# Casting V in the DMA, regrouping q and k as 64 rows of nine tokens, and a new order of loads in an attention and SwiGLU kernel

## Chip, cores and metric

One NeuronCore of one Trainium2 chip. The metric is device time in microseconds (us) of the whole launch, lower is better.

## What is computed

Causal attention with a selective bias, for 8 batches of 8 heads, 576 tokens and head size 64, and then a SwiGLU feed-forward block (FFN) on the 4608 rows that come out:

```python
cum  = np.cumsum(np.maximum(s, 0.0), axis=-1)
bias = -(cum[:, :, :, None] - cum[:, :, None, :])
scores = q @ k.T / sqrt(64) + minimum(bias, 0)     # causal
attn = softmax(scores) @ v                         # (8, 8, 576, 64)
x = attn.transpose(0, 2, 1, 3).reshape(4608, 512)
g = x @ w_gate                                     # 512 x 1536
out = (g * sigmoid(g) * (x @ w_val)) @ w_out       # 1536 x 512
```

Inputs and output are float32; the kernel multiplies in bfloat16.

## The kernel before

Heads are worked in 16 half-batches of four. For each, k and q are loaded, cast to bfloat16, and turned so that the head dimension lies on partitions. Half-batches 0 to 4 are turned by TensorE. From half-batch 5 on they go through scratch buffers in memory and a transposing DMA. Four small bias copies per half-batch (from the tile HL into the tiles KQ) add the rows that carry the cumulative sum. Scores of a head cannot start before its q, its k and its bias copy are all in KQ.

```python
J = 6                      # tokens per row: 576 = 96 rows of 6
NP = S // J                # partitions used by a q or k tile
def load_one(hb, name):    # hb: half-batch
    t = raw.tile([NP, HB, J, D], FP32, tag="raw" + name)          # two buffers
    nc.sync.dma_start(t, SRC[name][0][b, g*HB:(g+1)*HB].rearrange("h (p j) d -> p h (j d)", j=J))
def cast_one(hb, name, r, eng): ...        # NP x (2 heads * J * 64), float32 to bfloat16
def pe_transpose(hb, name, r, engs):
    for j in range(J):
        nc.tensor.transpose(ps[:, j, :], ct[:, r, j]..., ident[0:NP, 0:NP])
    # two copies from PSUM into KQ
...
nc.sync.dma_start(s_sb, ...); load_qk(0); load_qk(1); load_v(0, range(5))     # SyncE's queue
for r in range(NR): cast_one(0, "k", r, nc.gpsimd)                             # first casts on Pool
for r in range(NR): cast_one(0, "q", r, nc.gpsimd)
aug(0, [nc.scalar, nc.gpsimd, nc.scalar, nc.gpsimd])                           # bias copies
...
def side(h, step):         # called in the middle of each head; h is the half-batch
    ...                    # h == 0, step 3: load_qk(2)
    if h >= 2 and h + 3 < NHB and step == 0: load_qk(h + 3)
    ...                    # V: load on SyncE, cast on Pool, one batch ahead
# in attn_items, for half-batches 2, 3 and 4:
    if h > 3: aug(h, SP4)                      # bias copies of half-batch 4 are queued here
    for nm in ("k", "q"): cast_one(h, nm, 0, nc.gpsimd)
    ...                                        # then the transposes, then the heads
hook = {21: [lambda: load_qk(4)]}              # half-batch 4 is loaded late, by the first FFN tile
```

Batch 0 runs alone up to the "FFN start". After that the FFN of each batch's rows is woven between the heads of later ones; its first tile takes heads 8 to about 17. In the profile PE is TensorE, DVE VectorE, ACT ScalarE, POOL GpSimd (called Pool here) and SP SyncE; tps are TensorE's transposes, sc the scores, av the PV products, and pg, pv and py the FFN's gate, value and output products; ck and cq are the cast tiles, ks and qs the scratch buffers.

The softmax here doesn't subtract the row's maximum and nothing guards it: scores larger than these inputs give would overflow.

Of the kernel before, what the change touches and what calls it, by code (L numbers as in the profile page):

```python
# [12 lines left out]
FP32 = mybir.dt.float32  # L13
# [6 lines left out]
def kernel(  # L20
# [23 lines left out]
    J = 6  # L44
# [4 lines left out]
    WCH = 384  # L49
# [40 lines left out]
    WO = [const.tile([128, 3, DM], BF16, name=f"wo{j}") for j in range(4)]  # L90
# [12 lines left out]
    with tc.manual_schedule():  # L103
# [17 lines left out]

        def load_v(b, cs):
            if 0 in cs:
                loaded["v", b] = raw.tile([128, NCH, H, D], FP32, tag="rawv", bufs=1, name="rawv")
            t = loaded["v", b]
            for c in cs:
                n = 128 if c < 4 else TAIL
                nc.sync.dma_start(
                    t[0:n, c, :, :],
                    v[b, :, c * 128 : c * 128 + n, :].rearrange("h p d -> p h d"),  # L130
                )

        nc.sync.dma_start(s_sb, s.rearrange("b h n -> (b h) n"))
        load_qk(0)
        load_qk(1)
        load_v(0, range(5))

        PAIR_ONE = 1.0019378662109375
# [6 lines left out]
        nc.scalar.activation(warm, warm, AF.Exp)  # L145
        make_identity(nc, ident)
        nc.vector.memset(one_s, 1.0)
        nc.vector.memset(HL[:, 2:4, 0, :].bitcast(FP32), -1.005844116210937500)
        nc.vector.memset(HL[:, 0:2, 1, :].bitcast(FP32), PAIR_ONE)
        for e in range(2):  # L150
            nc.gpsimd.memset(aug_rows(0, e)[:, 1, :], PAIR_ONE)
            nc.vector.memset(aug_rows(0, e)[:, 0, :], 0.0)
        nc.gpsimd.memset(aug_rows(1, 0)[:, 1, :], PAIR_ONE)

# [4 lines left out]
        nc.vector.tensor_copy(HL[:, 2:4, 1, :], HL[:, 0:2, 0, :])  # L159

# [61 lines left out]
        def cast_v(b, c, eng):  # L222
            n = 128 if c < 4 else TAIL
            eng.tensor_copy(VT[b % 2][0:n, c, :, 0:D], loaded["v", b][0:n, c, :, :])  # L224

        def w_load(kind, j):
            dst = {"g": WG, "v": WV, "o": WO}[kind][j]
            if kind == "o":
                src_ap = moe_w_out[j * 384 : (j + 1) * 384, :].rearrange(
# [79 lines left out]
        def x_pe(pr):  # L309
# [16 lines left out]
            1: ("g", 2), 2: ("v", 2), 3: ("g", 3), 4: ("v", 3),  # L326
            5: ("o", 0), 6: ("o", 1), 7: ("o", 2), 8: ("o", 3),
        }

        def side(h, step):  # L330
# [3 lines left out]
            if h == 0:  # L334
                if step == 0:
                    for r in range(NR):
                        cast_one(1, "k", r, nc.gpsimd)
                        cast_one(1, "q", r, nc.gpsimd)
                if step == 1:
                    for nm in ("k", "q"):  # L340
                        pe_transpose(1, nm, 0, (nc.vector, nc.vector))
                if step == 2:
                    for nm in ("k", "q"):
                        pe_transpose(1, nm, 1, (nc.vector, nc.vector))
                if step == 3:
                    for c in range(5):
                        cast_v(0, c, nc.vector)
                    load_qk(2)
                return
            if h == 1:  # L350
                if step == 0:
                    aug(2, SP4)
                    load_v(1, range(5))
# [20 lines left out]
            if bn < B:  # L374
                if h % 2 == 0:
                    if step == 2:
                        load_v(bn, (0, 1))
                    if step == 3:
                        load_v(bn, (2, 3, 4))
                else:  # L380
                    if step == 1:
                        cast_v(bn, 0, nc.gpsimd)
                        cast_v(bn, 1, nc.gpsimd)
                    if step == 2:
                        cast_v(bn, 2, nc.gpsimd)
                        cast_v(bn, 3, nc.gpsimd)
                    if step == 3:
                        cast_v(bn, 4, nc.gpsimd)
# [174 lines left out]
```

## Time and profile before

| | before |
|---|---|
| time, median (range) of 3 runs | 427.5 us (427.38 to 428.12) |
| span of the profiled execution, granted clock | 425.2 us, 0.984 |
| first scores / first PV product / FFN start | 16.3 / 27.7 / 45.5 us |
| first gate product of the second FFN tile | 106.4 us |
| from there to the end | 318.8 us |

The prediction below shows how the page, the windows and the chain lead to these anchors. The last two rows cut the rest: "middle" is FFN start to the second FFN tile's first gate product (pg), "tail" is what follows.

### The profile page before, as it was taken

The page shows a single profiled execution, that of the slowest core. Times are in us where ns is not written, and L with a number is a line of the kernel's source. Part 1 is how long each engine was busy: PE and PEld are TensorE (multiplying, and loading weights), DVE is VectorE, ACT ScalarE, POOL GpSimd, SP SyncE. Part 2 cuts the span into 40 slices and gives each one's busy share as a digit, 9 for nine tenths or more (in the row PEclk, how much of TensorE's full clock was granted, in tenths as well). Part 3 has the DMA queues.
Part 4 walks back from the last instruction along what each step waited for, and adds up shares of the span by engine and source line. Part 5 has one row for each costly group of instructions (what it writes and reads, how often), then busy time and mean ns, then how long its engine had stood idle before and what let it go on. Part 6 is the DMA issues. An engine that isn't in the chain of part 4 may idle for free.

```text
span 425.2 us, 8041 instructions
## 1 busy us (share of the span) xinstructions
PE 387.1 (91%) x3058; PEld 215.3 (51%) x3112; DVE 255.1 (60%) x502; ACT 208.3 (49%) x418; POOL 142.1 (33%) x255
## 2 busy tenths in 40 slices
PE   1487788978999999999999999999999999999996
PEld 1265445545555555555555555555555554444442
DVE  7485558551697369636963796378637651861760
ACT  1454375654555455545554555555555642333321
POOL 5978133552335333533443344334411110000000
PEclk9999799997999999999999999999999999999999
DMA  8999998475796678467956994784720002002002
GB/s 191 205 244 195 199 227 179 94 209 151 165 198 114 175 194 192 105 188 172 207 101 190 185 199 102 186 183 90 105 83 2 2 25 76 0 2 100 2 1 99
DMA packets 92943, 56.71 MB, mean 133 GB/s; under 512 B 65600, under 2 KB 88208, under 8 KB 92904
## 3 DMA queue, kind: packets, MB, share of 16 engines
q1 hardware_dynamic: 86864, 51.40, 53.5%
q0 software_dynamic: 6016, 4.78, 7.0%
q8 instruction: 24, 0.39, 0.4%
q14 instruction: 15, 0.12, 0.1%
q10 hardware_dynamic: 24, 0.02, 0.0%
HBM read 37.90 MB, written 15.93 MB: 127 GB/s over the span
## 4 chain that ended last, share of the span: by engine, by line
PE 87%; DVE 4%; DMA 4%; issue 2%; ACT 1%; POOL 1%; SPq 0%; ACTq 0%
PE py L467 22%; PE pg L443 22%; PE pv L456 21%; PE sc L253 10%; PE av L286 8%; DVE kq L220 3%; PE xps L318 3%; DMA kq<-HL 2%; DMA rawq<-in_q_dram 2%; ACT pt L261 1%; DVE ot L302 1%; POOL cq L177 0%; DVE pp L450 0%; ACT th L448 0%; DVE rc L301 0%
## 5 line engine op out<-in xcount | busy, mean ns | idle before, releaser
L261 ACT ACTIVATE pt<-sc 128x512 bf16<-128x512 f32 (+1 forms) x256 | 117.5, 505 | 60.6 <-PE sc L253 60.3
L450 DVE SCALAR_TENSOR_TENSOR pp<-th,pg 128x512 bf16<-128x512 bf16 x108 | 74.1, 686 | 61.9 <-ACT th L448 61.5
L443 PE MATMUL pg<-xt,wg 128*128 128x512 bf16 x414 | 109.8, 381 | 1.3 <-issue 0.3
L456 PE MATMUL pv<-xt,wv 128*128 128x512 bf16 x412 | 109.6, 380 | 1.0
L448 ACT ACTIVATE th<-pg 128x512 bf16<-128x512 f32 x108 | 64.5, 597 | 92.5 <-PE pg L443 91.8
L467 PE MATMUL py<-wo,ht 128*128 128x512 bf16 x416 | 104.9, 383 | 1.0 <-issue 0.2
L253 PE MATMUL sc<-kq 128*128 128x128 bf16 (+4 forms) x576 | 77.7, 251 | 12.6 <-DVE kq L503 4.7
L265 POOL TENSOR_SCALAR_AFFINE_SELECT pt<-pt 128x512 bf16<-128x512 bf16 x64 | 40.6, 635 | 130.1 <-ACT pt L261 129.8
L461 DVE TENSOR_TENSOR ht<-pp,pv 128x512 bf16<-128x512 bf16 x108 | 73.9, 684 | 8.5 <-PE pv L456 0.9
L253 PEld LDWEIGHTS <-kq 128*128 128x128 bf16 x576 | 47.6, 102 | 46.8 <-issue 8.5
L467 PEld LDWEIGHTS <-ht 128*128 128x128 bf16 x432 | 38.5, 99 | 35.8 <-issue 1.1
L456 PEld LDWEIGHTS <-wv 128*128 128x128 bf16 x432 | 38.7, 98 | 35.2 <-issue 0.8
L443 PEld LDWEIGHTS <-wg 128*128 128x128 bf16 x432 | 38.3, 98 | 35.6 <-issue 0.5
L286 PE MATMUL av<-vt,pt 128*128 128x65 bf16 x960 | 51.4, 198 | 4.0 <-DVE ot L302 2.7
L286 PEld LDWEIGHTS <-pt 128*128 128x128 bf16 x960 | 42.6, 100 | 24.5 <-issue 5.0
L475 ACT ACTIVATE ysb<-py 128x512 f32<-128x512 f32 x36 | 21.5, 597 | 47.1 <-PE py L467 46.0
L270 POOL TENSOR_SCALAR_AFFINE_SELECT pt<-pt 128x64 bf16<-128x64 bf16 x64 | 15.3, 240 | 60.9 <-ACT pt L261 60.8
L301 DVE RECIPROCAL rc<-av 128x5 f32<-128x5 f32 x64 | 12.1, 189 | 37.5 <-PE av L286 37.5
L302 DVE TENSOR_TENSOR ot<-av,rc 128x320 bf16<-128x320 f32 x64 | 31.4, 491 | 2.2
L322 DVE COPY xt<-xps 128x64 bf16<-128x64 bf16 (+7 forms) x32 | 9.7, 304 | 37.3 <-PE xps L318 37.3
L177 POOL CAST ck<-rawk 96x768 bf16<-96x768 f32 x32 | 26.1, 835 | 3.6 <-DMA rawk<-in_k_dram 3.6
L224 POOL CAST vt<-rawv 128x512 bf16<-128x512 f32 (+1 forms) x35 | 23.0, 675 | 9.8 <-DMA rawv<-in_v_dram 9.8
(42 smaller groups left out, 168.6 us busy)
## 6 DMA issues: line engine op xcount, KB each, us to landing
rawk<-in_k_dram SPq DMA_DIRECT2D x16, 576.0 KB
rawq<-in_q_dram SPq DMA_DIRECT2D x16, 576.0 KB
out_dram<-ysb SPq DMA_DIRECT2D x36, 256.0 KB
rawv<-in_v_dram SPq DMA_DIRECT2D x32, 256.0 KB
ks<-ck SPq DMA_DIRECT2D x11, 288.0 KB
qs<-cq SPq DMA_DIRECT2D x11, 288.0 KB
wg<-in_moe_w_gate_dram POOLq DMA_DIRECT2D x4, 384.0 KB, 9.9
wv<-in_moe_w_val_dram POOLq DMA_DIRECT2D x4, 384.0 KB, 11.4
```

What stands on the lines that cost most here:

```text
L177: eng.tensor_copy(cts[name, hb][:, r].rearrange("p j e d -> p e j d"), loaded[name, hb][:, 2 * r : 2 * r + 2, :, :],)
L253: nc.tensor.matmul(sc[:, o : o + w], T[:, 0, r * S + 128 * tj : r * S + 128 * (tj + 1)], T[:, 1, r * S + lo : r * S + hi], start=True, sto ...
L261: nc.scalar.activation(pt[:, CHUNK_PT[ci] : CHUNK_PT[ci] + o], sc[:, 0:o], AF.Exp, scale=0.125)
L265: nc.gpsimd.affine_select(pt[:, 1088:1600], pt[:, 1088:1600], pattern=[[0, 4], [1, 128]], compare_op=ALU.is_ge, fill=zreg, base=0, channel ...
L286: nc.tensor.matmul(av[:, bi * (D + 1) : (bi + 1) * (D + 1)], pt[:, c0 : c0 + 128], VT[b % 2][:, tj, h, :], start=(tj == 0), stop=(tj == bi),)
L302: nc.vector.tensor_mul(ot[:, :, e * D : (e + 1) * D], av3[:, :, 0:D], rc[:, :, None].to_broadcast([128, NCH, D]),)
L443: nc.tensor.matmul(pg, WG[j][:, c, f0 : f0 + 128], xt[:, c, :], start=(c == 0), stop=(c == 3),)
L448: nc.scalar.activation(th, pg, AF.Tanh, scale=0.5)
L450: nc.vector.scalar_tensor_tensor(pp, in0=th, scalar=1.0, in1=pg, op0=ALU.add, op1=ALU.mult)
L456: nc.tensor.matmul(pv, WV[j][:, c, f0 : f0 + 128], xt[:, c, :], start=(c == 0), stop=(c == 3),)
L461: nc.vector.tensor_mul(ht, pp, pv)
L467: nc.tensor.matmul(py, hts[ft][:, ts_ * 128 : (ts_ + 1) * 128], WO[ft // 3][:, ft % 3, :], start=(ft == 0), stop=(ft == NFT - 1),)
```

## The change

The intent: take V's casts from the engines and V's loads from SyncE's queue, move fewer and longer descriptors for q and k, free the bias copies from waiting behind Pool's casts, and have the first casts done by an engine that is idle at that moment.

```diff
-    J = 6
+    J = 9
-    WCH = 384
+    WCH = 768
         def load_v(b, cs):
-                nc.sync.dma_start(
-                    t[0:n, c, :, :],
+                nc.gpsimd.dma_start(
+                    VT[b % 2][0:n, c, :, 0:D],          # casts on the way
@@ start @@
-        load_qk(0)
+        load_first()                                    # k and q by pairs of heads
         load_qk(1)
-        load_v(0, range(5))
@@ side(), half-batch 0 @@
-                if step == 0: (casts of half-batch 1 on gpsimd)
+                if step < 2:  (casts of half-batch 1 on vector)
-                    load_qk(2)
@@ attn_items @@
                 if first and bh == H:
+                    aug(3, SP4)
+                    load_qk(2)
                     load_qk(3)
-                    aug(3, SP4)
@@ prologue @@
-            cast_one(0, "k", r, nc.gpsimd)
+            cast_act("k", r)                            # ScalarE
+            cast_act("q", r)
-        aug(0, [nc.scalar, nc.gpsimd, nc.scalar, nc.gpsimd])
+        aug(0, [nc.gpsimd] * 4)
-        aug(1, [nc.gpsimd] * 4)
+        aug(1, SP4)
+        load_v(0, range(5))
@@ weaving @@
-            n0 = 0
+            n0 = 6 if tt == 0 else 0                    # six FFN units before head 8
```

(Cut to its core; parenthesised lines sum up several. WCH is the number of columns in one piece of the FFN's weights, SP4 is SyncE's queue for all four bias copies that `aug` issues, and a step is a quarter of a half-batch, one head. The cut leaves out that the weights' pieces are also issued at other heads.)

More of the change, by code (lines that the diff above doesn't have):

```diff
@@ L48 @@
     NFT = DF // 128
-    WCH = 384
+    WCH = 768
+    WKO = 6
     NWCH = DF // WCH
@@ L89 @@
     WV = [const.tile([128, 4, WCH], BF16, name=f"wv{j}") for j in range(NWCH)]
-    WO = [const.tile([128, 3, DM], BF16, name=f"wo{j}") for j in range(4)]
+    WO = [const.tile([128, WKO, DM], BF16, name=f"wo{j}") for j in range(NFT // WKO)]
     KQ = [
@@ L120, in load_qk, with load_first @@
             load_one(hb, "q")
+        def load_first():
+            for name in ("k", "q"):
+                loaded[name, 0] = raw.tile([NP, HB, J, D], FP32, tag="raw" + name, name="raw" + name)
+            for r in range(NR):
+                for name in ("k", "q"):
+                    nc.sync.dma_start(
+                        loaded[name, 0][:, 2 * r : 2 * r + 2, :, :],
+                        SRC[name][0][0, 2 * r : 2 * r + 2, :, :].rearrange(
+                            "h (p j) d -> p h (j d)", j=J
+                        ),
+                    )
         def load_v(b, cs):
-            if 0 in cs:
-                loaded["v", b] = raw.tile([128, NCH, H, D], FP32, tag="rawv", bufs=1, name="rawv")
-            t = loaded["v", b]
             for c in cs:
                 n = 128 if c < 4 else TAIL
-                nc.sync.dma_start(
-                    t[0:n, c, :, :],
+                nc.gpsimd.dma_start(
+                    VT[b % 2][0:n, c, :, 0:D],
                     v[b, :, c * 128 : c * 128 + n, :].rearrange("h p d -> p h d"),
@@ L133 @@
         nc.sync.dma_start(s_sb, s.rearrange("b h n -> (b h) n"))
-        load_qk(0)
+        load_first()
         load_qk(1)
-        load_v(0, range(5))
-        PAIR_ONE = 1.0019378662109375
+        ONES2 = 1.0019378662109375
+        NEGS2 = -1.0058441162109375
         def aug_rows(i, e):
@@ L145 @@
         nc.scalar.activation(warm, warm, AF.Exp)
+        nc.vector.memset(one_s, 1.0)
+        nc.vector.memset(HL[:, 2:4, 0, :].bitcast(FP32), NEGS2)
+        nc.vector.memset(HL[:, 0:2, 1, :].bitcast(FP32), ONES2)
         make_identity(nc, ident)
-        nc.vector.memset(one_s, 1.0)
-        nc.vector.memset(HL[:, 2:4, 0, :].bitcast(FP32), -1.005844116210937500)
-        nc.vector.memset(HL[:, 0:2, 1, :].bitcast(FP32), PAIR_ONE)
         for e in range(2):
-            nc.gpsimd.memset(aug_rows(0, e)[:, 1, :], PAIR_ONE)
-            nc.vector.memset(aug_rows(0, e)[:, 0, :], 0.0)
-        nc.gpsimd.memset(aug_rows(1, 0)[:, 1, :], PAIR_ONE)
+            nc.gpsimd.memset(aug_rows(0, e)[:, 1, :], ONES2)
+            nc.gpsimd.memset(aug_rows(0, e)[:, 0, :], 0.0)
+            nc.scalar.copy(
+                KQ[1][e][64 * (1 - e) : 64 * (1 - e) + 64, 1, :],
+                one_s[:, 0:1].to_broadcast([64, NR * S + 64]),
+            )
+        nc.vector.memset(aug_rows(1, 0)[:, 0, :], 0.0)
         nc.vector.tensor_scalar(s_sb, s_sb, 0.0, 8.0, ALU.max, ALU.mult)
@@ L159 @@
         nc.vector.tensor_copy(HL[:, 2:4, 1, :], HL[:, 0:2, 0, :])
+        for e in range(2):
+            for i in range(2):
+                nc.vector.memset(KQ[i][e][64 * e : 64 * e + 64, :, NR * S :], 0.0)
         def aug(hb, engs):
@@ L220, in pe_transpose @@
                     engs[e].tensor_copy(dst, srcp)
-        def cast_v(b, c, eng):
-            n = 128 if c < 4 else TAIL
-            eng.tensor_copy(VT[b % 2][0:n, c, :, 0:D], loaded["v", b][0:n, c, :, :])
         def w_load(kind, j):
@@ L228, in w_load @@
             if kind == "o":
-                src_ap = moe_w_out[j * 384 : (j + 1) * 384, :].rearrange(
+                src_ap = moe_w_out[j * WKO * 128 : (j + 1) * WKO * 128, :].rearrange(
                     "(c p) n -> p c n", p=128
@@ L325 @@
         wlate = {
-            1: ("g", 2), 2: ("v", 2), 3: ("g", 3), 4: ("v", 3),
-            5: ("o", 0), 6: ("o", 1), 7: ("o", 2), 8: ("o", 3),
+            0: ("g", 0), 1: ("v", 0), 2: ("g", 1), 3: ("v", 1), 6: ("o", 0), 7: ("o", 1),
         }
@@ L334, in side @@
             if h == 0:
-                if step == 0:
-                    for r in range(NR):
-                        cast_one(1, "k", r, nc.gpsimd)
-                        cast_one(1, "q", r, nc.gpsimd)
-                if step == 1:
+                if step < 2:
                     for nm in ("k", "q"):
-                        pe_transpose(1, nm, 0, (nc.vector, nc.vector))
-                if step == 2:
+                        cast_one(1, nm, step, nc.vector)
                     for nm in ("k", "q"):
-                        pe_transpose(1, nm, 1, (nc.vector, nc.vector))
-                if step == 3:
-                    for c in range(5):
-                        cast_v(0, c, nc.vector)
-                    load_qk(2)
+                        pe_transpose(1, nm, step, (nc.vector, nc.vector))
                 return
@@ L352, in side @@
                     aug(2, SP4)
+                    init_vt(1)
+                if step == 1:
                     load_v(1, range(5))
@@ L373, in side @@
             bn = h // 2 + 1
-            if bn < B:
-                if h % 2 == 0:
-                    if step == 2:
-                        load_v(bn, (0, 1))
-                    if step == 3:
-                        load_v(bn, (2, 3, 4))
-                else:
-                    if step == 1:
-                        cast_v(bn, 0, nc.gpsimd)
-                        cast_v(bn, 1, nc.gpsimd)
-                    if step == 2:
-                        cast_v(bn, 2, nc.gpsimd)
-                        cast_v(bn, 3, nc.gpsimd)
-                    if step == 3:
-                        cast_v(bn, 4, nc.gpsimd)
+            if bn < B and h % 2 == 1:
+                if step == 0:
+                    load_v(bn, (0, 1))
+                if step == 1:
+                    load_v(bn, (2, 3, 4))
         def attn_items():
@@ L403, in attn_items @@
                         cast_one(h, nm, 1, nc.gpsimd)
-                    if h == 2:
-                        for c in range(5):
-                            cast_v(1, c, nc.gpsimd)
                     yield kk + 0.01
@@ L468, in ffn_items @@
                         py, hts[ft][:, ts_ * 128 : (ts_ + 1) * 128],
-                        WO[ft // 3][:, ft % 3, :],
+                        WO[ft // WKO][:, ft % WKO, :],
                         start=(ft == 0), stop=(ft == NFT - 1),
@@ L479, in ffn_items, with cast_act, init_vt @@
                 yield 1
-        for r in range(NR):
-            cast_one(0, "k", r, nc.gpsimd)
-        for r in range(NR):
-            cast_one(0, "q", r, nc.gpsimd)
-        aug(0, [nc.scalar, nc.gpsimd, nc.scalar, nc.gpsimd])
-        nc.gpsimd.memset(aug_rows(1, 1)[:, 1, :], PAIR_ONE)
-        for e in range(2):
-            nc.vector.memset(aug_rows(1, e)[:, 0, :], 0.0)
-        pe_transpose(0, "k", 0, (nc.scalar, nc.scalar))
-        pe_transpose(0, "k", 1, (nc.scalar, nc.scalar))
-        pe_transpose(0, "q", 0, (nc.vector, nc.vector))
-        pe_transpose(0, "q", 1, (nc.vector, nc.vector))
-        w_load("g", 0)
-        w_load("v", 0)
-        aug(1, [nc.gpsimd] * 4)
-        w_load("g", 1)
-        w_load("v", 1)
-        for i in range(2):
-            nc.vector.memset(VT[i][:, :, :, D : D + 1], 1.0)
-            nc.vector.memset(VT[i][64:128, 4, :, 0:D], 0.0)
-        for e in range(2):
-            for i in range(2):
-                nc.vector.memset(KQ[i][e][64 * e : 64 * e + 64, :, NR * S :], 0.0)
+        def cast_act(name, r):
+            if r == 0:
+                cts[name, 0] = cp.tile([NP, NR, J, 2, D], BF16, tag="c" + name, bufs=2, name="c" + name)
+            nc.scalar.copy(
+                cts[name, 0][:, r].rearrange("p j e d -> p e j d"),
+                loaded[name, 0][:, 2 * r : 2 * r + 2, :, :],
+            )
+        def init_vt(i):
+            nc.gpsimd.memset(VT[i][:, :, :, D : D + 1], 1.0)
+            nc.gpsimd.memset(VT[i][64:128, 4, :, 0:D], 0.0)
+        for r in range(NR):
+            cast_act("k", r)
+            cast_act("q", r)
+        aug(0, [nc.gpsimd] * 4)
+        for nm in ("k", "q"):
+            pe_transpose(0, nm, 0, (nc.vector, nc.vector))
+        for nm in ("k", "q"):
+            pe_transpose(0, nm, 1, (nc.vector, nc.vector))
+        nc.vector.memset(aug_rows(1, 1)[:, 0, :], 0.0)
+        aug(1, SP4)
+        init_vt(0)
+        load_v(0, range(5))
         at = attn_items()
```

## The prediction

> **What bounds the kernel now.** I read the page's forty slices first, then ten-microsecond windows, then the chain of waits and the timeline of the first 100 us, and last the waits by line. From the page of the kernel before:
>
> ```profile
> PE   1487788978999999999999999999999999999996
> DVE  7485558551697369636963796378637651861760
> POOL 5978133552335333533443344334411110000000
> PEclk9999799997999999999999999999999999999999
> DMA  8999998475796678467956994784720002002002
> ```
>
> From slice 11 on (about 106 us) TensorE is full; Pool and VectorE never are. What can be won lies in the first ten slices. The windows say how much:
>
> ```profile
> 0.00:10.00 10.00, 1.32 (x12) 0.90 (x12) 7.76 (x13) 1.49 (x2) 5.18 (x12) 1.00 0.79 187
> 10.00:20.00 10.00, 3.89 (x27) 2.45 (x27) 4.55 (x12) 5.31 (x10) 9.33 (x15) 1.00 1.26 210
> 40.00:50.00 10.00, 7.49 (x69) 4.77 (x71) 4.29 (x12) 1.19 (x2) 2.65 (x4) 0.66 1.20 204
> 50.00:60.00 10.00, 7.42 (x61) 4.25 (x62) 5.88 (x10) 7.14 (x14) 4.32 (x8) 1.00 1.07 215
> 70.00:80.00 10.00, 7.48 (x77) 4.62 (x77) 6.52 (x12) 7.29 (x14) 3.63 (x6) 1.00 0.51 120
> 90.00:100.00 10.00, 5.93 (x54) 3.73 (x53) 4.25 (x8) 4.74 (x9) 3.19 (x5) 0.76 0.65 171
> 200.00:300.00 100.00, 99.16 (x830) 55.75 (x845) 69.16 (x139) 55.38 (x115) 39.19 (x70) 1.00 0.71 157
> ```
>
> The first two numbers are the stretch and TensorE's busy time in it. In the first 50 us TensorE idles 21.4 us (50 less 1.32, 3.89, 7.89, 8.03 and 7.49); three later windows lose 2.6, 2.5 and 4.1; the hundred from 200 lose 0.8. The last three columns (granted clock, DMA share, GB/s) show the DMA engines saturated at the start. The chain of waits through the start, cut:
>
> ```profile
> 2.09 7.16 DMA rawq<-in_q_dram
> 10.84 6.13 DMA kq<-HL
> 19.47 0.78 POOL ck L177
> 20.97 0.02 issue
> 21.00 0.75 DVE kq L220
> 27.17 0.90 DVE vt L224 x2
> 28.11 0.33 PE av L286 x3
> 45.18 0.33 issue
> 45.52 1.49 PE pg L443 x3
> ```
>
> Three anchors follow: the bias copy (kq<-HL) lands at 16.97 and holds the Pool queue and the first heads; the second half-batch (heads 4 to 7) runs through Pool casts, transposes and VectorE copies from 19.5 to 27; the first PV product starts at 27.7, the FFN at 45.5. From there to 425.2 is 379.7 us, nearly all TensorE.
>
> **What the Trainium skill says.** "DMA: Bandwidth & Descriptors", section "SWDGE vs HWDGE vs iDMA": only GpSimd's queue casts during a DMA. The weights already do this here. "Perfetto Trace Analysis", section "DMA Instruction — SWDGE (GPSIMD)": the recorded length of a Pool DMA is descriptor generation, not the movement. The trace agrees: wg issues take a median of 0.77 us and land after 9.9. "SBUF — State Buffer", section "Door 1: The DMA port swizzle": partitions 0 to 63 reach only 8 of 16 ports, measured there at 196 GB/s for 1 MiB. The 96-row loads here run at 245 to 257 GB/s (windows from 4 to 12 us); a 64-row load has no run yet. "TensorE: Matmul & The Clock Gate", Part 1: an idle array drops to half clock and needs about 3.4 us of work to recover. The trace agrees: the granted clock is 0.50 from 42 to 46 us, where TensorE waits for VectorE between PV products.
>
> **The change part by part.**
>
> 1. V by a casting Pool DMA. It removes 35 Pool casts (23.0 us) and 5 VectorE casts (1.9 us) and takes 40 DMAs off SP. Only two of these are near the path: the VectorE casts at 27.17 and the second batch's Pool casts, which waited 9.8 us for their data and put the ninth head's mask behind them (54.35 us). It adds 40 issues to Pool. A 64-descriptor bias issue takes 0.60, a 384- or 512-descriptor weight issue 0.75 to 0.82; the slope is about 0.4 ns a descriptor, so 1024 descriptors cost about 1.0 us (estimate). Five in a row are 5 us, in steady state two and then three in heads that last 5.3 us. Beside the head's 0.63 + 0.24 us of masks and two casts (below, 2.4 us) the fullest head's Pool has 6.3 us of work. Its last mask is needed about 8 us after its first starts, so this should stay hidden.
>
> 2. 64 rows of nine. A Pool cast goes from 768 to 1152 elements: 0.82 to about 1.2 us. 56 remain of 64, so Pool's cast time rises from 52 to about 67 us, less V's 23: net nothing. TensorE transposes per tile go from 6 to 9. In the busy stage six take about 0.26 us start to start; nine are about 0.36. Twelve such tiles fall in the FFN stage: **+1.2 us**.
>
> 3. Bias copies on Pool, V out of the way. HL is ready at 8.2 us. Issued at 8.3 with the shortest landing seen (5.6 us), the first lands near 14 instead of 16.97: the first scores start about **2.5 us earlier** than 16.3. This is not a gain at the end yet, since the built order puts the next half-batch's transposes after only half of head 0 (before: half of head 1).
>
> 4. First casts on ScalarE, second half-batch's on VectorE. The second q load must land first. 2.51 MB lie up to it (0.15 + 4 x 0.295 + 2 x 0.59). At 200 GB/s (the skill's port limit, as estimate) from 2.3 us that is 14.9; some 1.9 us to landing and a little sharing with V give 17. A VectorE cast of 1152 elements, scaled from 0.415 us for 512, is about 0.86. From 17: q cast to 17.9, four copies of 0.77 to 21.0, two casts to 22.7, transposes of row two to 23.8. Then 2.5 heads of exps at 4 x 0.46 = 1.84 us give 28.4 for the first PV product, against 27.74: **+0.7**. At 245 GB/s the load lands 2.3 us sooner: -1.6. I take the middle, **-0.4**.
>
> 5. From first PV product to FFN the same work follows (17.8 us: heads 4 to 7, then PV products one by one through a single PSUM buffer). Weights in larger pieces move the same bytes. The built program makes each Pool DMA wait for the eighth Pool DMA before it; so w_out's second piece waits for the second gate piece. With V at 12 to 23 us and each 1.57 MB piece at about 5 us (estimate from 786 KB in 32 descriptors of 78 ns, twice over) that one lands near 38, where head 7 is: hardly a wait. **0**.
>
> 6. Six FFN units first (n0 = 6). q/k of half-batch 2 are now issued only after head 7's scores (about 37 to 39 us, before at 16.4). They land near 46 and 51, the Pool casts end near 54; TensorE gets to their transposes at about 46 + 7.7 = 53. The gap of 2.6 us there may close or grow. With V off SP and off Pool, the waits at 50 to 60 and at 96 (2.9 us for kq<-HL behind SP's transposes) should on average lose half: 2.6 + 4.1 = 6.7, so **-3.3**.
>
> Sum: +1.2 - 0.4 + 0 - 3.3 = -2.5 us, so 427.5 becomes **425.0 us**.
>
> **The rivals.** (a) The start is bound by the new order, not by the bias copy: TensorE stalls inside head 0 until the 64-row q load, VectorE's four casts and copies pass in series, and the FFN starts at 46 or later. For: VectorE holds 12.2 us of copies and casts there. It gives 427 to 431. (b) Late q/k of half-batch 2: loads started at 39 us share the engines with V and w_out; each us late is a TensorE us and the clock drops as well. It gives 430 to 434. (c) Casting V is slow per descriptor (256 B read, 128 B written) or costs Pool over 2 us an issue: then masks come late in seven batches, some 2 us each, and the time is 435 to 440. The weight issues speak against it, but none has 1024 descriptors. (d) The start was held by DMA saturation: V out of the first 11 us and bigger descriptors free everything, first PV product near 25 and two of the three later gaps close: 425.2 - 2.7 - 6 on the trace, so about 418.
>
> **Range and chances.** (a), (b) and the central case lie within 2% (419.0 to 436.1); (d) alone reaches below, (c) alone above. The reserve is at most some 30 us of idle, most of it in chains that the change keeps. 80% range: 416 to 433. Faster by over 2%: 0.22; within: 0.70; slower: 0.08.
>
> **What would show it.** Right: first scores at 13 to 15 us, hb1's VectorE casts waiting for the q load at 15 to 18, first PV product at 26 to 29, FFN start at 44 to 47, V issues on Pool near 1 us, no rise of TensorE idle after 110 us. Wrong: FFN start below 42 (then the start was bound by DMA), Pool waiting for earlier Pool DMAs over 3 us before a mask, V issues of 2 us or more, or transposes of half-batch 2 waiting over 3 us for Pool casts.

## The result, and the profile after

The changed kernel took **431.08 us** (430.41 to 431.71, 4 runs) against 427.76 us for the kernel before in the same rounds. The ratio is 1.0077, with a 95% interval of 1.0059 to 1.0096: 3.3 us. Ratios here are the mean time of one kernel's fast runs over the mean of the other's of the same rounds, so not quite the ratio of the medians quoted. The forecast was a ratio of 0.994: the size lies inside its range, the sign is wrong.

The windows of the kernel after, to hold against those of the prediction (stretch, TensorE busy first, granted clock, DMA share and GB/s last):

```profile
50.00:60.00 10.00, 7.25 (x61) 3.75 (x61) 6.21 (x9) 5.32 (x10) 4.19 (x5) 0.83 1.17 234
90.00:100.00 10.00, 5.67 (x70) 3.49 (x68) 3.45 (x7) 2.96 (x6) 5.28 (x7) 0.86 1.19 202
200.00:300.00 100.00, 99.12 (x826) 55.50 (x838) 67.99 (x136) 56.00 (x116) 45.36 (x68) 1.00 0.88 142
```

The gaps at 50 and at 90 are still there; the first has a lower granted clock (0.83 for 1.00). The hundred from 200 are as before (99.12 for 99.16). The chain of waits names what holds the start and the two gaps:

```profile
8.00 8.70 DMA kq<-HL
36.90 15.22 DMA rawq<-in_q_dram
89.89 6.24 DMA rawq<-in_q_dram
100.04 2.14 DMA kq<-HL
```

The first line is a bias copy that takes 8.70 us from issue to landing at 16.70; the second a q load of half-batch 2 that is issued at 36.90 and lands at 52.1; the last two the q load and the bias copy of half-batch 4. TensorE's timeline of the kernel after (start, duration, what, and in brackets the idle time before with its releaser):

```profile
27.74 1.01 PE L300 MATMUL av<-vt,pt 128*128 128x65 bf16 x15
...
43.85 1.49 PE L437 MATMUL pg<-xt,wg 128*128 128x512 bf16 x3 [0.33 <-DMA vt<-in_v_dram]
...
53.37 0.43 PE L227 MATMUL tps<-ident,cq 64*128 64x64 bf16 x9 [1.21 <-POOL cq L195]
...
97.44 0.66 PE L227 MATMUL tps<-ident,cq 64*128 64x64 bf16 x9 [3.46 <-POOL cq L195]
...
102.22 1.46 PE L267 MATMUL sc<-kq 128*128 128x128 bf16 x8 [1.94 <-DMA kq<-HL]
...
111.05 0.81 PE L437 MATMUL pg<-xt,wg 128*128 128x512 bf16 x3
```

and the two of the kernel before that answer to the last two:

```profile
96.71 1.46 PE L253 MATMUL sc<-kq 128*128 128x128 bf16 x8 [2.86 <-DMA kq<-HL]
...
106.42 0.81 PE L443 MATMUL pg<-xt,wg 128*128 128x512 bf16 x3
```

Read in order: the first PV product starts at 27.74 us in both. The FFN starts 1.7 us earlier (43.85 for 45.52). Head 16, the first of half-batch 4, starts 5.5 us later, and the second FFN tile 4.6 us later. From there on both need 319 us (318.8 and 318.95). So in these two executions the change wins 1.7 us up to the FFN start and then loses 6.3 us in the 60 us of the middle. Nothing is lost in the tail. The sum, 4.8 us between the spans, is more than the 3.3 us of the timed runs, because the profiled execution of the kernel after is the slowest of its four (431.71 us) and that of the kernel before (426.86 us) is a fast one; the split is that of one execution of each.

Two groups of the page after and one of before show what the layout does to Pool (count, then busy time and mean ns of one):

```profile
L195 POOL CAST ck<-rawk 64x1152 bf16<-64x1152 f32 x28 | 32.7, 1186 | 8.3 <-DMA rawk<-in_k_dram 8.3
L138 POOL DMA_DIRECT2D vt<-in_v_dram x40 | 33.9, 862 | 2.1 <-DMA kq<-HL 2.1
```

```profile
L177 POOL CAST ck<-rawk 96x768 bf16<-96x768 f32 x32 | 26.1, 835 | 3.6 <-DMA rawk<-in_k_dram 3.6
```

### The profile page after: what moved, and what is told of

The parts are those of the page before. It is cut to its first block, busy times and chain, and to the rows that moved or that the text cites. A ratio compares the mean times of both kernels' runs of the same rounds, so it can differ in the third digit from the quotient of the medians.

```text
span 430.0 us, 8118 instructions
## 1 busy us (share of the span) xinstructions
PE 390.3 (91%) x3118; PEld 215.8 (50%) x3172; DVE 258.4 (60%) x499; ACT 212.5 (49%) x420; POOL 162.2 (38%) x248
## 4 chain that ended last, share of the span: by engine, by line
PE 79%; DMA 8%; DVE 5%; POOL 3%; ACT 2%; issue 1%; SPq 0%; ACTq 0%; DVEq 0%; POOLq 0%
PE py L461 20%; PE pg L437 20%; PE pv L450 20%; PE sc L267 10%; PE av L300 6%; DMA rawq<-in_q_dram 5%; DMA kq<-HL 3%; PE xps L332 2%; ACT pt L275 2%; POOL cq L195 2%; POOL ck L195 1%; DVE kq L238 1%; DVE pp L444 1%; DVE kq L217 1%; DMA s_sb<-in_s_dram 1%
## 5 line engine op out<-in xcount | busy, mean ns | idle before, releaser
L275 ACT ACTIVATE pt<-sc 128x512 bf16<-128x512 f32 (+1 forms) x256 | 117.8, 505 | 62.7 <-PE sc L267 62.3
L437 PE MATMUL pg<-xt,wg 128*128 128x512 bf16 x415 | 111.2, 384 | 1.4 <-DMA vt<-in_v_dram 0.3
L450 PE MATMUL pv<-xt,wv 128*128 128x512 bf16 x412 | 111.1, 384 | 1.3
L444 DVE SCALAR_TENSOR_TENSOR pp<-th,pg 128x512 bf16<-128x512 bf16 x108 | 74.1, 686 | 62.3 <-ACT th L442 61.8
L442 ACT ACTIVATE th<-pg 128x512 bf16<-128x512 f32 x108 | 64.5, 597 | 90.9 <-PE pg L437 90.9
L279 POOL TENSOR_SCALAR_AFFINE_SELECT pt<-pt 128x512 bf16<-128x512 bf16 x64 | 40.8, 637 | 114.6 <-ACT pt L275 114.6
L267 PEld LDWEIGHTS <-kq 128*128 128x128 bf16 x576 | 47.2, 102 | 43.2 <-issue 8.7
L315 DVE RECIPROCAL rc<-av 128x5 f32<-128x5 f32 x64 | 12.1, 190 | 40.5 <-PE av L300 40.4
L195 POOL CAST ck<-rawk 64x1152 bf16<-64x1152 f32 x28 | 32.7, 1186 | 8.3 <-DMA rawk<-in_k_dram 8.3
L138 POOL DMA_DIRECT2D vt<-in_v_dram x40 | 33.9, 862 | 2.1 <-DMA kq<-HL 2.1
L195 POOL CAST cq<-rawq 64x1152 bf16<-64x1152 f32 x28 | 31.5, 1150 | 6.0 <-DMA rawq<-in_q_dram 6.0
```

What stands on the lines that cost most here:

```text
L138: nc.gpsimd.dma_start(VT[b % 2][0:n, c, :, 0:D], v[b, :, c * 128 : c * 128 + n, :].rearrange("h p d -> p h d"),)
L195: eng.tensor_copy(cts[name, hb][:, r].rearrange("p j e d -> p e j d"), loaded[name, hb][:, 2 * r : 2 * r + 2, :, :],)
L267: nc.tensor.matmul(sc[:, o : o + w], T[:, 0, r * S + 128 * tj : r * S + 128 * (tj + 1)], T[:, 1, r * S + lo : r * S + hi], start=True, sto ...
L275: nc.scalar.activation(pt[:, CHUNK_PT[ci] : CHUNK_PT[ci] + o], sc[:, 0:o], AF.Exp, scale=0.125)
L279: nc.gpsimd.affine_select(pt[:, 1088:1600], pt[:, 1088:1600], pattern=[[0, 4], [1, 128]], compare_op=ALU.is_ge, fill=zreg, base=0, channel ...
L437: nc.tensor.matmul(pg, WG[j][:, c, f0 : f0 + 128], xt[:, c, :], start=(c == 0), stop=(c == 3),)
```

## Theories, and the experiments

**T1**: the loads of half-batches 2 and 4 come late (q/k of 2 queued behind head 7's bias copies; q of 4 waits for the raw buffer of half-batch 5). **T2**, formed after the first four runs: what sets half-batch 4 is the time at which half-batch 5's casts end, because SyncE's in-order queue then has scratch writes, two transposing DMAs and an output write before half-batch 4's bias copies. SyncE's queue in the kernel after shows what T2 means (start, and for how long the queue is held):

```profile
96.66 1.26 SPq L212 DMA_TRANSPOSE pk<-ks  x1
98.03 1.29 SPq L212 DMA_TRANSPOSE pq<-qs  x1
100.04 2.84 SPq L183 DMA_DIRECT2D kq<-HL  x4
```

The rivals: **R1**, V cast on the Pool queue is the cost. **R2**, the rows of nine are (slower loads, longer casts, more transposes). **R3**, the six FFN units ahead of head 8 are.

All runs in one table, cut where the profile was cut above (profiled execution of each; the ratio is from the timed runs; "rows" is tokens per row):

| run | rows | FFN start | middle | tail | ratio to before [95%] |
|---|---|---|---|---|---|
| before | 6 | 45.5 | 60.9 | 318.8 | 1 |
| after | 9 | 43.9 | 67.2 | 319.0 | 1.0077 [1.0059, 1.0096] |
| q/k of 2 early | 9 | 43.4 | 65.6 | 319.0 | 1.0054 [1.0025, 1.0084] |
| loads of 4 and 6 exchanged | 9 | 42.6 | 64.1 | 319.0 | 1.0065 [1.0018, 1.0112] |
| both | 9 | 43.1 | 66.3 | 319.0 | 1.0057 [1.0028, 1.0086] |
| no six FFN units first | 9 | 43.9 | 69.6 | 319.0 | 1.0129 [1.0085, 1.0173] |
| bias copies of 4 early | 9 | 43.5 | 62.7 | 319.1 | 1.0009 [0.9981, 1.0036] |
| all three order edits | 9 | 43.3 | 59.6 | 319.3 | 0.9939 [0.9906, 0.9972] |
| rows of six | 6 | 41.6 | 61.8 | 318.1 | 0.9922 [0.9894, 0.9950] |
| rows of six and all three | 6 | 40.8 | 57.9 | 318.1 | **0.9792** [0.9763, 0.9820] |
| V on SyncE, queued late | 9 | 55.9 | 63.7 | 321.9 | 1.0387 [1.0346, 1.0428] |
| V on SyncE, queued first | 9 | 43.7 | 74.3 | 322.0 | 1.0379 [1.0349, 1.0408] |
| before, rows of nine | 9 | 47.8 | 61.9 | 322.1 | 1.0174 [1.0131, 1.0217] |
| before, bias of 4 early | 6 | 44.9 | 58.2 | 318.9 | 0.9899 [0.9864, 0.9934] |
| half-batch 1 behind the bias | 9 | 55.3 | 64.5 | 318.9 | 1.0318 [1.0289, 1.0348] |
| q on the upper partitions | 9 | 42.8 | 64.7 | 319.0 | 1.0044 [1.0013, 1.0076] |
| the same, q on ScalarE's queue | 9 | 43.2 | 64.9 | 318.9 | 1.0072 [1.0039, 1.0105] |

One warning on its columns: the profiled execution is one of four, and these differ by 1 to 4 us. The exchange of loads is the worst case: its profiled run, 427.40 us, was its fastest, the others took 429.3 to 431.6. Differences of under 1 us between rows are not read here. Where the record of a tile's first gate product is missing from the trace (a group of three instead of four, as before and after), the start stands up to 0.4 us late. All outputs were correct.

### Loads earlier (T1)

```diff
 # e2: q/k of half-batch 2 in head 0 instead of behind head 7's bias copies
+                if step == 1:
+                    load_qk(2)
...
-                    load_qk(2)
 # e3: half-batch 4 takes the raw buffer that is free, 6 the late one
-                load_qk(h + 3)
+                load_qk(4 if h == 3 else h + 3)
-            21: [lambda: load_qk(4)],
+            21: [lambda: load_qk(6)],
 # e6: both
```

> The changed kernel with one edit: half-batch 2's q/k loads are queued on SP right after the second half-batch's bias copies (head 1), not after head 7's bias copies. Theory T1 (loads of half-batches 2 and 4 arrive late): q of half-batch 2 lands before 45 us instead of 52.1, TensorE's waits for the Pool casts at 51.7 to 55.6 (1.21 + 0.66 + 0.66 us and more in the weight-load row) vanish, time falls by 2 to 3.5 us to about 428. Rival R1 (casting V on the Pool queue is the cost): no change beyond 0.5 us. Rival R2 (the 64-row layout, slower casts and more transposes): no change beyond 0.5 us.

> The changed kernel with one edit: the loads of half-batches 6 and 4 trade places in the ring of raw buffers, so that 4 takes the buffer freed at 75 us and not the one freed only when Pool has cast q of half-batch 5 (89.8 us). T1: Pool no longer waits for rawq at 93 to 96 us (3.2 us), TensorE's stop between 93.9 and 102.2 us shrinks by 3 to 4 us and less time is spent at half clock: about 427. R1: gain below 1 us, because Pool stays behind with V issues. R2: gain below 1 us.

> Both edits at once. T1: the gains add up, 5.5 to 7.5 us, to about 424.5, so below the kernel before (the FFN starts 1.7 us sooner than in it). R1 and R2: not below 429.

Measured: 429.46, 430.05 and 429.39 us. Loading half-batch 2 early does take the wait at 53 us away (its transposes then run from 52.0 to 53.4), but little time goes with it: by the ratios 1.0 and 0.5 us for the two edits and 0.9 us for both, none of them clear of the noise, since the intervals overlap with that of the kernel after. The exchange takes away the wait for q of half-batch 4, and TensorE's timeline of that run shows what comes in its place:

```profile
92.68 0.43 PE L227 MATMUL tps<-ident,cq 64*128 64x64 bf16 x9 [0.66 <-POOL cq L195]
98.59 1.46 PE L267 MATMUL sc<-kq 128*128 128x128 bf16 x8 [5.48 <-DMA kq<-HL]
```

The transposes end 7 us earlier than in the kernel after (92.68 for 99.63 for the last start), and the scores stand 5.48 us for the bias copy. The gain was turned into a new wait. T1 is right on the waits and wrong on what they are worth; T2 was formed from this line.

### The six FFN units (R3)

```diff
-            n0 = 6 if tt == 0 else 0
+            n0 = 0
```

> The changed kernel without the six FFN units that come first (n0 = 0). T1: TensorE now meets half-batch 2's transposes some 5 us sooner, while its q still lands at about 52 us, so the wait there grows by 3 to 5 us; half-batch 5's casts come sooner, so the stop at half-batch 4 shrinks by 2 to 3: net 0 to +3 us, 431 to 434. Rival R3 (the six units themselves are the cost): back to 428 or less.

Measured: 432.99 us. Taking them away does not bring the time back to 428 or less, as R3 asked, so R3 falls. The middle is longer (69.6 for 67.2 us), as T1 said, but this execution is the slowest of its four (434.26), and the intervals of the two ratios overlap: that the six units cover part of the late loads is likely, not shown.

### Bias copies of half-batch 4 early (T2)

```diff
+            if h == 3 and step == 0:
+                aug(4, SP4)
...
-                    if h > 3:
-                        aug(h, SP4)
```

> The changed kernel with one edit: half-batch 4's bias copies are queued on SP at head 12 (their rows are free then) and not behind half-batch 5's two transposes. T2: head 16's first scores no longer wait for kq<-HL (1.94 us), only for the late casts; first scores at 100 to 101 us instead of 102.2: 1 to 2.5 us less, 428.5 to 430. R1, R2: under 1 us.

> All three order edits at once (half-batch 2's loads early, half-batch 4's loads in an earlier buffer, its bias copies early). T2: the stop at half-batch 4 shrinks from 8.3 us to 3 to 4, less time at half clock, total 5 to 7 us less: 424 to 426, below the kernel before. R1 and R2: not below 428.

Measured: 427.22 us for this edit alone, a little better than expected, and 423.98 us for all three order edits together. In the latter, no wait is left in front of head 16 on TensorE's timeline:

```profile
95.34 1.46 PE L267 MATMUL sc<-kq 128*128 128x128 bf16 x8
```

It starts 6.9 us earlier than in the kernel after (102.22), and the middle is 7.6 us shorter. The edit of the bias copies alone wins 2.9 us of the ratio (1.0077 to 1.0009). The two edits of the loads, which alone brought nothing clear of the noise, bring 3.0 us more once it is in place (1.0009 to 0.9939; which of the two was not tried). T2 holds: in an in-order queue it is the last of several waits that pays, and the bias copies were the last.

### Rows of six again (R2)

```diff
-    J = 9
+    J = 6
```

> The changed kernel with 96 rows of six tokens again (one constant). R2 (the 64-row layout is the cost): Pool casts take 0.82 us and not 1.14, so the transposes of half-batches 2, 3 and 4, which the casts pace (waits of 0.66 us a tile), lose about 1 us less each; q casts of half-batch 5 end about 2 us sooner and head 16's first scores with them; 96-row loads land sooner: in sum 3 to 5 us less, 426 to 428. T2 (what counts is when half-batch 5's q casts end, since SP's queue then has scratch writes, two transposes and only then half-batch 4's bias copies) allows 2 to 3 us of it. R1 (V on Pool): under 1 us.

> The kernel before with one number changed: rows of nine tokens on 64 partitions (J = 9), nothing else of the change. If the layout itself is the loss (slower loads, casts 0.35 us longer each, three more transposes a tile): loads near 200 instead of 245 GB/s in the first 12 us, FFN start 2 to 3 us later than 45.5, half-batches 2 and 4 later by about 1 us each, 431 to 434 us. If the layout hurts only in the changed order (through the late loads of half-batches 2 and 4), it stays at 427 to 429 us.

> The changed kernel with rows of six again (J = 6, 96 partitions) and with all three edits of the order (q/k of half-batch 2 loaded in head 0, the loads of half-batches 4 and 6 exchanged, bias copies of half-batch 4 issued in head 12). If layout and order are two separate losses, this run has both gains: FFN start as with rows of six alone (41.6 us), no wait for a bias copy before head 16, second FFN tile from about 99 to 100 us instead of 103.4, and so 419 to 421 us in the median. If the two repair the same wait twice, it stays where either was alone, 423 to 424 us.

Measured: 423.50 us for the changed kernel with rows of six, 434.24 for the kernel before with rows of nine, and 417.87 for rows of six with all three order edits. The layout was expected to matter and mattered more. Put back in the changed kernel, rows of six win 1.55 points of the ratio (1.0077 less 0.9922), 6.6 us. Put into the kernel before, rows of nine lose 1.7 points, 7.4 us. The single number J outweighs the whole loss of the change: R2 holds, beside T2. Where it works shows in the first windows, before with rows of six and then of nine:

```profile
4.00:8.00 4.00, 0.03 (x1) 0.04 (x2) 3.86 (x6) 0.00 (x0) 1.06 (x2) 1.00 1.07 253
8.00:12.00 4.00, 2.61 (x24) 1.76 (x24) 2.44 (x5) 1.70 (x3) 3.61 (x5) 1.00 1.08 246
```

```profile
4.00:8.00 4.00, 0.00 (x0) 0.00 (x0) 3.86 (x6) 0.00 (x0) 0.88 (x1) 1.00 1.04 219
8.00:12.00 4.00, 1.97 (x27) 1.50 (x27) 1.75 (x4) 1.35 (x3) 3.52 (x4) 1.00 1.05 202
```

The DMA engines at nearly the same share of busy time (1.04 to 1.08) move 253 and 246 GB/s into 96 partitions and 219 and 202 into 64. By the table the layout costs 2.3 to 2.6 us up to the FFN start in all three pairs (before, after, and with the order edits), or 1.9 to 2.7 us with the missing records allowed for. In the middle it costs 1.0 us in the kernel before, 1.7 us with the order edits, and 5.4 us in the changed order. That last figure must not be read as late loads and slow casts making each other dearer: by the timed runs the layout costs 6.6 us in the changed order and 6.3 us with the order edits (0.9939 less 0.9792), the same within the noise. In the tail it costs 0.8 to 1.2 us where V is cast by the DMA and 3.3 us in the kernel before. There the waits by line say which:

```profile
PE pv L456 <- DVE pp L450: 3.0, 5, 0.6
```

five waits of 0.6 us of TensorE for VectorE's product, 3.0 us; no such wait is listed for the kernels before and after. The two runs below that put V back on SyncE, also with rows of nine, list the same five waits (3.1 us) and have the same longer tail. The timeline shows what VectorE does just before such a wait:

```profile
129.01 3.04 DVE L199 COPY kq<-pq 64x1152 bf16<-64x1152 bf16 x2
```

These copies take 0.93 us in the mean in this run (0.95 with V back on SyncE, 0.79 in the kernel before, 0.82 after), and Pool is casting k and V beside them here. That Pool's casts make them longer was not tested.

The run with both repairs is the best of all, 2.1% under the kernel before, though the interval reaches to 1.8%. Its expectation had put the question whether layout and order are two losses (419 to 421 us) or one wait repaired twice (423 to 424). They are two: rows of six win 1.55 points of the ratio, the order edits 1.38, both together 2.85, almost the sum. Its 417.87 us is better than either version that this study was about.

### V back on SyncE (R1)

```diff
-                nc.gpsimd.dma_start(VT[b % 2][0:n, c, :, 0:D], ...)
+                nc.sync.dma_start(t[0:n, c, :, :], ...)        # t: float32, one buffer
+    (casts as before: batch 0 on VectorE, the others on Pool)
 # e4: batch 0 queued where the changed kernel has it; f4: directly behind load_qk(1)
```

> The changed kernel with V loaded by SP as float32 and cast by VectorE (first batch) and Pool (the rest) as in the kernel before. R1 (V by casting Pool DMA is the cost): 3 us or more are won, 428 or less. T2: Pool's three V issues in a row (2.5 us) put the q casts of half-batch 5 back by about 1.3 us, which comes back, but the first PV products wait for five VectorE casts again (+0.6 to 1.5 us): 429 to 432.

> As the run with V on SP and cast by the engines, but with the first batch's V queued directly behind the q/k loads, as in the kernel before, and not behind the bias copies of half-batch 1. If that run's 12 us were only the late V of the first batch (it lost them before the FFN start and none after), the FFN starts near 46 us and the time is 431 to 434 us: V by a casting DMA is then worth 0 to 3 us here. If V on SP costs by itself in every batch, 437 us or more.

Measured: 443.07 and 442.70 us, both far beyond what was expected, and for different reasons. In the first, batch 0's V is queued behind half-batch 1's bias copies and the FFN starts 12 us late. The second cures that (FFN start 43.7), and loses the time in the middle instead. SyncE's timeline, then TensorE's:

```profile
28.80 20.45 SPq L141 DMA_DIRECT2D rawv<-in_v_dram  x5
```

```profile
58.94 0.66 PE L235 MATMUL tps<-ident,ck 64*128 64x64 bf16 x9 [6.85 <-POOL ck L203]
```

The five V loads of batch 1 hold SyncE's queue from 28.80 to 49.25, and the q/k loads of half-batch 2, behind them in this order, are issued at 52.27 and come 7 us late. The kernel before has the same hold, from 29.08 for 17.87 us, but has queued q/k of half-batch 2 ahead of it. So the cost looks like one of the order, though no run moves these loads alone, and the runs do not give a price of V's cast by itself in the middle. In the tail they do, with rows of nine: 322.0 for 319.0 us, so V cast in the DMA is worth 3 us there. With rows of six no run undoes it alone. R1 falls: where these runs price that part of the change, it is a gain.

### The kernel before with one order edit

```diff
 # kernel before
+            if h == 3 and step == 0:
+                aug(4, SP4)
...
-                    if h > 3:
-                        aug(h, SP4)
```

> The kernel before with the bias copies of half-batch 4 issued in head 12 instead of behind the transposes of half-batch 4, nothing of the change. The first scores of head 16 waited 2.86 us for the bias copy in the kernel before; if SP's order holds them there too, the wait goes and the time falls by 2 to 3 us to 423.5 to 425. If the transposes are what really comes last, less than 1 us: 426 to 427.5.

Measured: 422.43 us, better than expected. By the ratio that is 4.3 us. In the profiled execution, the slowest of the four (423.76), the wait at head 16 is gone and the middle falls by 2.7 us, about the 2.86 us of that wait; what the rest is was not looked for. This wait was in the profile of the kernel before all along, and two moved lines are worth more than the change.

### Why the bias copies land late (step 3)

```diff
         load_first()
-        load_qk(1)
...
         aug(1, SP4)
+        load_qk(1)
```

> The changed kernel with the k/q loads of half-batch 1 queued on SP behind the bias copies of half-batch 1 instead of ahead of them. If the bias copies of half-batch 0 on the Pool queue land late (8.0 us after issue) because 1.2 MB of loads stand before them on the same DMA engines, they land at 11 to 13.5 us now and the first scores start there, not at 16.84; half-batch 1's loads land later in turn, so the first PV product may gain nothing: time 428 to 433. If 8 us is what such a copy takes on the Pool queue anyway, the first scores stay at 16 to 17 us.

Measured: 440.45 us. TensorE's timeline:

```profile
11.33 1.04 PE L266 MATMUL sc<-kq 128*128 128x128 bf16 x6
...
26.88 0.66 PE L226 MATMUL tps<-ident,ck 64*128 64x64 bf16 x9 [14.52 <-DVE ck L194]
```

The DMA issues of the kernel after, then of this run (KB each, median us from issue to landing):

```profile
kq<-HL POOLq DMA_DIRECT2D x4, 9.0 KB, 8.0
```

```profile
kq<-HL POOLq DMA_DIRECT2D x4, 9.0 KB, 1.9
```

With no loads ahead the same four copies on the same queue land in 1.9 us instead of 8.0, and the first scores start at 11.33. So it is the backlog of SyncE's loads that delays a small DMA of another queue. The price is larger than the gain: SyncE gets to half-batch 1's loads only at 16.69, behind bias copies of its own that hold its queue for 9.33 us, and TensorE then stands 14.5 us. The expectation had this cost far too small (428 to 433).

### Load rate or casts? (the roads of R2)

```diff
+        PS = {"k": slice(0, 64), "q": slice(64, 128)}
-            t = raw.tile([NP, HB, J, D], ...)
+            t = raw.tile([128, HB, J, D], ...)[PS[name]]       # same for the cast tile
-                    ps[:, j, :], ct[:, r, j]..., ident[0:NP, 0:NP]
+                    ps[:, j, :], ct[:, r, j]..., ident[PS[name], PS[name]]
 # g3 also: q of half-batches 0 and 1 by nc.scalar.dma_start
```

> The changed kernel with all of q (its raw tile, its cast and the left side of its transposes) on partitions 64 to 127, k on 0 to 63 as it was; casts, transposes and bytes the same. If only the partitions reached limit the loads and k and q overlap in the queue, the rate of the first 12 us rises from 200 towards 250 GB/s, the FFN starts near 42 us and the time is 425 to 428. If the queue works its transfers off one after the other, the rate stays at 200 GB/s and the time at 429 to 432.

> As the run before, with the q loads of half-batches 0 and 1 issued on ScalarE's queue, so that k and q run side by side from the start. If the 64 partitions are what limits a load, the rate of the first 12 us is 240 GB/s or more, half-batch 1's data lands about 2 us sooner, the first PV product starts near 26 and the FFN near 42 us: 425 to 429. If the limit lies elsewhere (the descriptors or the memory), the rate stays at 200 GB/s and nothing is gained: 430 to 433.

Measured: 428.64 and 429.60 us. The window from 6 to 10 us of the kernel after, of q on the upper half, and of the same with q on ScalarE's queue:

```profile
6.00:10.00 4.00, 1.39 (x20) 1.07 (x21) 3.75 (x9) 3.27 (x3) 2.00 (x4) 1.00 1.03 203
```

```profile
6.00:10.00 4.00, 1.89 (x27) 1.50 (x27) 3.79 (x10) 3.47 (x4) 1.98 (x4) 1.00 1.03 231
```

```profile
6.00:10.00 4.00, 1.32 (x18) 1.00 (x18) 3.12 (x10) 3.90 (x4) 1.45 (x3) 1.00 1.04 301
```

The rate rises with the partitions reached, from 203 to 231 GB/s, with the same bytes and from the same queue. The step to 301 GB/s comes with a second queue, whose share was not tried on its own. But the FFN starts only 0.7 to 1.0 us earlier. In the fastest case half-batch 1's casts on VectorE start at 15.70 us, directly behind its eight copies and a memset, and no longer wait for data. So at most about 1 us of the layout's 2.3 us at the start belongs to the rate, and even that is no more than these executions differ by. The rest goes with the tile's shape and was not split further; VectorE's casts are part of it (its q cast is 0.75 to 0.94 us for 64x1152 and 0.54 for 96x768). By the timed runs neither variant is clearly apart from the changed kernel: the intervals of the ratio overlap.

## Why the prediction was wrong, step by step

- **Step 1 held.** A V issue took 0.86 us on Pool (expected 1.0), and TensorE's waits for Pool's masks are as before, one of 1.0 us on its weight loads. But the step looked at masks alone: three issues (2.47 us from 84.38 us) stand ahead of the q casts of half-batch 5, which end at 89.86, just before the q load of half-batch 4 is issued at 89.89 (it waits for their buffer). What that costs was not split.
- **Step 2 failed; it is the largest miss.** "Net nothing" for Pool and +1.2 us for TensorE was a sum of busy time, and for Pool a wrong one: it leaves out the 40 V issues of step 1 (Pool's busy time rose from 142.1 to 162.2 us). TensorE paid nothing: nine transposes of 64 columns follow each other after 0.27 us and six of 96 after 0.26. Pool's cast, 1.15 to 1.19 instead of 0.83 us, stands in series before each of the four transposes of a half-batch, which are paced by it at 1.09 us, and the loads before it run at 203 instead of 250 GB/s. Measured: 6.6 us (rows of six put back) and 7.4 us (rows of nine alone). With rows of six the rest of the change wins 3.3 us (0.9922), close to the -3.7 us that the other steps add up to, but by luck: in the profiled execution the win lies before the FFN start (3.9 us), and the middle, where -3.3 was forecast, is 0.9 us longer.
- **Step 3 failed on the landing, not in the sum.** The copy was taken to land after 5.6 us, at 14; it landed at 16.7, with half-batch 1's loads ahead of it. Expected first scores at 14, measured 16.84. (The step also mixed two copies: the one that lands at 16.97 in the kernel before is not the one that head 0 waited for, since its scores start at 16.27.)
- **Step 4 was nearly right.** The load rate of 200 GB/s was right (203). That branch gave +0.7 for the first PV product, the middle that was forecast -0.4, and 0.0 was measured. (Scaled in proportion, its VectorE cast would have been 0.93 us and not 0.86; 0.75 to 0.94 was measured.) The path had one wait that the step lacked: half-batch 1's q landed at 16.4 (17 expected), but VectorE's copies then waited 1.34 us, to 18.48, for transposes that stand behind the first scores and so behind the bias copy of step 3.
- **Step 5 was off by 1.7 us to the good.** Before, the first PV product of the chain lies behind VectorE's V casts and runs slowly. The next two PV rounds then come after 2.8 and 2.9 us; in the kernel after it is 2.2 and 2.1. With V's casts back on VectorE but the rest of the new order (V queued first) the FFN still starts at 43.7. The casts alone are therefore not the cause.
- **Step 6 failed in sign.** "Should on average lose half" had no chain behind it. Predicted were -3.3 us for the middle; measured were +6.3 in the profiled executions, of which the three order edits give back 7.6, rows of six 5.4 and both together 9.3; in the timed runs the two gains add up (5.9, 6.6 and 12.1 us). The step timed the load of half-batch 2 well (q landed at 52.1, 51 expected; the last Pool cast ended at 55.5, 54 expected). It failed at half-batch 4: V's leaving SyncE's queue was to shorten the wait for the bias copy, but that copy still stands behind two transposes in the queue and lands at 102.2. There the q load, issued at 89.89, comes late as well (TensorE waits 3.46 us for its cast and 1.94 us for the copy).

Rival (b), late q/k of half-batch 2, named the right kind of cause and the right range (430 to 434), but the order edit that pays most on its own sat at half-batch 4, and rows of nine, which the rival does not name, cost more than the whole loss: that its number fits is partly luck. Rivals (a), (c) and (d) fall: the FFN starts at 43.9 and not at 46 or later, a V issue takes 0.86 us, and the first PV product does not come near 25. What stays open: which of the casts cost the rest at the start, what lengthens VectorE's copies in the tail of the kernel before with rows of nine, and V's price in the middle. The larger weight pieces, the first casts on ScalarE and VectorE and the new queues of the first bias copies were never undone on their own.

## What to carry to other kernels

A step that "costs nothing on an engine with idle time" must be checked for where it stands in series: a longer cast before each transpose can cost its whole length where its data is late. When a queue works in order, list what stands behind each wait in it before pricing that wait, and move the small copy that others need to the front. A change of many parts should be measured with each part undone (here not all were): one number cost more than the whole loss, and the other parts, freed of it and reordered, win 2.1%.

## What the Trainium skill lacked or had wrong

- "DMA: Bandwidth & Descriptors", section "Rules for kernel authors", says of two transfers to disjoint partition halves not to bother, because they serialize. Here q on partitions 64 to 127 beside k on 0 to 63 raised the rate from 203 to 231 GB/s from one queue and to 301 GB/s from two, though little of the time came with it. One transfer over all 128 partitions, which the page advises instead, was not tried.
- "DMA: Bandwidth & Descriptors", section "Queues, rings and completion order", describes the turns that queues take packet by packet, from which one might expect a small DMA of another queue to pass a backlog; it gives no figure for that. Here a 9 KB copy on Pool's queue took 1.9 us alone and 8.0 us behind SyncE's loads.
- No page was found with the cost of a tile's shape as a whole. The same bytes as 64 rows of nine and as 96 rows of six differ by 0.32 us per Pool cast (1.15 and 0.83 for q and k of the kernel before with J = 9 and with J = 6), by some 50 GB/s in loading, and by nothing in transposes; 7 us of the kernel's time hung on it.
